# Forming the cross-attention factor G in three runs of 1536 columns for two batches, in place of four runs

## The chip, the cores and the metric

One core of one Trainium2 chip. The metric is the time of one execution on the device, in microseconds; lower is better. Spans in profiles are some 1.8 us shorter than these times.

## The reference, cut to what matters

```python
B, H, S, Ns, D = 8, 8, 512, 32, 64          # x [B,H,S,D], state [B,H,Ns,D]
a     = softmax(x @ state.T / sqrt(D))       # over the 32 states
xread = a @ state                            # 512 rows a batch
a2    = softmax(state @ x.T / sqrt(D))       # over the 512 tokens
sread = a2 @ x                               # 32 rows a batch
y = concat(xread, sread) as [B*(S+Ns), H*D]  # 4352 x 512
out = max(y @ w1, y @ w2, y @ w3) @ w_out    # 512 -> 768 -> 512
```

The kernel never forms xread. It forms G = state x (w1, w2, w3) of a batch, 2304 columns wide, and multiplies the softmax weights with it.

## The kernel before: what the change and the argument touch

Per batch b there are six "maxouts" (`x_maxout(b, m)`, 128 of the 768 columns of the maximum in the reference, 6 matmuls of 512 columns each), four "output pieces" of the batch ahead (`ffn_out(b-1, j)`, the product with w_out, 6 matmuls each), scores and softmax of batch b+1, `sread(b+1)`, and G, whose matmuls use the array as 8 tiles of 64 rows by 32 columns. A group of G is 8 such matmuls of up to 512 columns; a run is a stretch of groups with no other matmuls between. VectorE takes its instructions in the order of the program (in the prediction's lines softmax's reduction, at 79.20, stands between the maxima of two maxouts). The matmuls write to PSUM, from which the other engines copy. The kernel's PSUM tiles share buffers by tag: "two" has 2 buffers of 128x1024, "pw" has 4 of 128x512. A new tile waits until the last reader of the older tile in its buffer has ended.

```python
def g_front(b):                      # 1280 columns, beside sread
    flush_copies()
    g_piece(b, 0, 512, act)          # tag "two", copied out by ScalarE
    g_piece(b, 512, 1024, act, True) # True: ScalarE copies it one maxout later
    g_piece(b, 1024, 1280, dve)      # two tiles of tag "pw", copied by VectorE

def g_back(b):                       # 1024 columns, by itself
    flush_copies()
    g_piece(b, 1280, 1792, act)
    g_piece(b, 1792, 2304, act, True)

def maxout(b, m, n, lhs, rhs, nk):   # three tiles of "pw", released by these readers:
    ...
    nc.scalar.copy(out=t0[:, 0:n], in_=pw[0][:, 0:n])
    if copies_due:
        copies_due.pop(0)()
    nc.vector.tensor_max(t1[:, 0:n], t0[:, 0:n], pw[1][:, 0:n])
    nc.vector.tensor_max(ht[b][:, m, :], t1[:, 0:n], pw[2][:, 0:n])

for b in range(2, B):                # maxout m, then slots[m] in order
    n = b + 1
    slots = [[] for _ in range(NM)]
    if n < B:
        slots[0].append(lambda: scores(n, 0, 2))
        slots[1].append(lambda: softmax(n, 0, 2, (nc.gpsimd.tensor_mul, J)))
        slots[1].append(lambda: x_pad(n))            # GpSimd, for sread
        slots[2].append(lambda: a_transpose_dma(n))
        ...                                          # (cut)
    slots[1].append(lambda: g_back(b))
    if n < B:
        slots[4].append(lambda: sread(n))
        slots[4].append(lambda: g_front(n))
    for j, m in enumerate((1, 2, 4, 5)):             # output pieces: last in 1, 2; first in 4, 5
        slots[m].insert(0 if m > 2 else len(slots[m]), lambda j=j: ffn_out(b - 1, j))
    for m in range(NM):
        x_maxout(b, m)
        for f in slots[m]:
            f()
```

Maxouts 0 and 1 read the columns 0 to 768 of G, maxouts 2 and 3 those from 768 to 1536, maxouts 4 and 5 the rest.

The softmax here doesn't subtract the row's maximum and nothing guards it: scores larger than these inputs give would overflow.

## Time and profile before

| | before |
|---|---|
| time, median of 3 runs | 154.67 us |
| steady batch, start to start of maxout 0 | 15.21 us |
| runs of G for batches 2 to 7 | 12, of which 6 by themselves |
| copies of G in these batches | ScalarE 24 of 128x1024, VectorE 12 of 128x256 |

The prediction below shows the lines. PE is TensorE, PEld its weight loads, DVE VectorE, ACT ScalarE, POOL GpSimd. In the lists in order of time a line has the start in us, the length, the engine, the line of the kernel, what is written and read, and how many instructions are merged; a bracket at the end is the idle time of that engine just before, and what ended it. For TensorE only starts are to be compared, as the ends overlap the next instructions.

### The profile page before, as it was taken

How to read it: one execution, taken by the hardware profiler on the slowest of the kernel's cores; microseconds unless marked ns; L12 is line 12 of the kernel's file. 1: busy time of each engine (PE TensorE's matmuls, PEld its weight loads, DVE VectorE, ACT ScalarE, POOL GpSimd, SP SyncE). 2: the span in 40 equal slices, each digit the busy share in tenths (PEclk: the TensorE clock that was granted, in tenths of full speed). 3: DMA queues.
4: the chain of work that ended last, by engine and by line, in shares of the span. 5: the costliest groups of instructions: out<-in, count | busy, mean ns of one | idle time of the engine just before them, and what ended most of it. 6: DMA issues, size and time to landing. Idle time of an engine off the chain costs nothing.

```text
span 153.1 us, 3479 instructions
## 1 busy us (share of the span) xinstructions
PE 145.3 (95%) x1370; PEld 71.3 (47%) x1386; DVE 97.9 (64%) x177; ACT 93.9 (61%) x145; POOL 66.5 (43%) x80
## 2 busy tenths in 40 slices
PE   6988999999999999999999999999999999999990
PEld 2536543554453445344534453445344555665450
DVE  3477868768827685768576767776767684565110
ACT  3656878686948656865686568656865646333340
POOL 8977899754421782078308310821082100101050
PEclk9999999999999999999999999999999999999999
DMA  5999999999929999999496963061206120210374
GB/s 109 214 171 203 194 167 110 206 234 186 260 45 219 157 129 253 194 127 199 170 179 81 193 162 137 9 202 43 104 17 194 52 97 0 94 45 0 141 248 163
DMA packets 37376, 21.85 MB, mean 143 GB/s; under 512 B 22512, under 2 KB 35056, under 8 KB 37360
## 3 DMA queue, kind: packets, MB, share of 16 engines
q0 software_dynamic: 17184, 14.94, 52.4%
q1 hardware_dynamic: 19888, 6.43, 23.0%
q10 hardware_dynamic: 288, 0.26, 0.6%
q8 instruction: 11, 0.18, 0.5%
q14 instruction: 5, 0.04, 0.1%
HBM read 15.20 MB, written 8.91 MB: 158 GB/s over the span
## 4 chain that ended last, share of the span: by engine, by line
PE 84%; DMA 5%; POOL 4%; ACT 2%; issue 2%; DVE 0%; POOLq 0%
PE pw L373 44%; PE po L411 28%; DMA w<-in_moe_w_dram 5%; PE pg L301 4%; POOL w L109 2%; PE ps L200 2%; PE psr L267 2%; PE pg L327 2%; POOL x L80 2%; ACT G L333 1%; PE ph L403 1%; ACT t L377 1%; DVE t L380 0%; PE pat L231 0%; PE pxt L178 0%
## 5 line engine op out<-in xcount | busy, mean ns | idle before, releaser
L373 PE MATMUL pw<-aT,G 128*128 128x512 bf16 x288 | 69.0, 379 | 0.2 <-ACT G L333 0.2
L380 DVE TENSOR_TENSOR t<-t,pw 128x512 bf16<-128x512 bf16 (+1 forms) x54 | 35.1, 650 | 29.7 <-ACT t L377 29.6
L411 PE MATMUL po<-wout,ht 128*128 128x512 bf16 x183 | 46.6, 379 | 1.0 <-DVE t L380 0.2
L373 PEld LDWEIGHTS <-G 128*128 128x128 bf16 x288 | 26.8, 98 | 32.1 <-issue 2.7
L381 DVE TENSOR_TENSOR ht<-t,pw 128x512 bf16<-128x512 bf16 (+1 forms) x54 | 35.5, 658 | 5.6
L414 ACT COPY osb<-po 128x512 f32<-128x512 f32 x33 | 19.4, 586 | 29.6 <-PE po L411 29.6
L377 ACT CAST t<-pw 128x512 bf16<-128x512 f32 (+1 forms) x54 | 30.5, 565 | 10.4 <-PE pw L373 9.7
L411 PEld LDWEIGHTS <-ht 128*128 128x128 bf16 x198 | 18.8, 98 | 23.9 <-issue 2.8
L425 POOL DMA_DIRECT2D out_dram<-osb x14 | 7.9, 566 | 46.5 <-ACT osb L414 32.1
L220 POOL TENSOR_TENSOR a<-e,rden 128x1024 bf16<-128x1024 bf16 (+2 forms) x10 | 15.3, 1531 | 26.0 <-DVE rden L215 15.9
L308 ACT CAST G<-pg 128x1024 bf16<-128x1024 f32 x24 | 24.5, 1021 | 2.3 <-PE pg L301 1.5
L246 POOL COPY xp<-x 128x2048 bf16<-128x2048 bf16 x6 | 11.3, 1881 | 0.0
L213 DVE TENSOR_REDUCE den<-e 128x32 f32<-128x1024 bf16 (+1 forms) x10 | 9.9, 995 | 0.8 <-ACT e L205 0.8
L333 ACT CAST G<-pg 128x768 bf16<-128x768 f32 x11 | 8.7, 808 | 2.0 <-PE pg L327 2.0
L109 POOL DMA_DIRECT2D w<-in_moe_w_dram x12 | 9.2, 783 | 1.0 <-DVE rden L215 1.0
L373 PE MATMUL pw<-ats,w 128*128 128x256 bf16 x72 | 8.8, 273 | 0.0
L205 ACT ACTIVATE e<-ps 128x1024 bf16<-128x1024 f32 x6 | 6.2, 1029 | 3.7 <-PE ps L200 3.7
L127 PE MATMUL idle<-zero 128*128 128x512 bf16 x19 | 6.9, 512 | 1.2 <-DVE zero L85 1.2
L373 PEld LDWEIGHTS <-w 128*128 128x128 bf16 x72 | 7.0, 98 | 2.1
L301 PE MATMUL pg<-w,bd 64*32 64x512 bf16 x192 | 7.5, 381 | 0.0
L153 POOL COPY bd<-stT 64x512 bf16<-64x512 bf16 x6 | 6.5, 1082 | 0.9 <-DMA stT<-st 0.7
L200 PEld LDWEIGHTS <-xT 128*128 128x128 bf16 x128 | 5.0, 98 | 2.2 <-ACT xT L182 0.3
(61 smaller groups left out, 86.1 us busy)
## 6 DMA issues: line engine op xcount, KB each, us to landing
out_dram<-osb POOLq DMA_DIRECT2D x14, 512.0 KB, 3.2
x<-in_x_dram POOLq DMA_DIRECT2D x6, 512.0 KB, 9.2
w<-in_moe_w_dram POOLq DMA_DIRECT2D x6, 256.0 KB, 6.5
x<-in_x_dram POOLq DMA_DIRECT2D x3, 256.0 KB, 6.8
w<-in_moe_w_dram POOLq DMA_DIRECT2D x6, 128.0 KB, 7.0
wout<-in_moe_w_out_dram POOLq DMA_DIRECT2D x1, 768.0 KB, 11.1
x0f<-in_x_dram SPq DMA_DIRECT2D x1, 512.0 KB
out_dram<-osb SPq DMA_DIRECT2D x1, 512.0 KB, 2.7
```

Source lines behind the costliest of these rows:

```text
L109: nc.gpsimd.dma_start(out=w_slices(w_sb, c)[:, :, i, :], in_=w[:, :, m0 * 128:m1 * 128])
L220: mul(out=a[b][:, r, g0:g1].rearrange("p j g s n -> p j (g s) n"), in0=e[b][:, r, g0:g1].rearrange("p j g s n -> p j (g s) n"), in1=rden[: ...
L246: nc.gpsimd.tensor_copy(out=x_pads[b % 2][:, 2:2 + 2 * H * PW].rearrange("p (k c) -> p k c", c=PW)[:, :, 0:2 * D], in_=x_sb[b][:, 0:XW].re ...
L301: nc.tensor.matmul(ps[g][32 * s:32 * s + 32], bd(b, 2 * s + g)[64 * g:64 * g + 64, g, :], w_sb[64 * g:64 * g + 64, s, c0:c1], start=True, ...
L308: copy(out=G[b][:, :, c0:c1], in_=p[:, :, 0:n])
L333: copy(out=m_cols(G[b], m), in_=pv)
L373: nc.tensor.matmul(p[:, 0:n], lhs(i, k), rhs(k), start=(k == 0), stop=(k == nk - 1))
L377: nc.scalar.copy(out=t0[:, 0:n], in_=pw[0][:, 0:n])
L380: nc.vector.tensor_max(t1[:, 0:n], t0[:, 0:n], pw[1][:, 0:n])
L381: nc.vector.tensor_max(ht[b][:, m, :], t1[:, 0:n], pw[2][:, 0:n])
L411: nc.tensor.matmul(p, ht[b][:, m, j * 128:(j + 1) * 128], wout_sb[:, m, :], start=(m == 0), stop=(m == NM - 1))
L414: act(out=o[:, j, :], in_=p)
```

## The change

The intent: each change of TensorE between full-array matmuls and tiles of 64 by 32 costs time, so form G in runs as long as these buffers allow, 1536 columns, and need nine runs for six batches in place of twelve. The core of the diff (the body of the matmul loop, unchanged in substance, is cut):

```diff
+    def g_run(now, later, *split):
+        flush_copies()
+        for b, c0, c1 in (now, later):        # two tiles of tag "two", ScalarE copies
+            ...                               # (cut) `later` one maxout later
+        ps = [pp.tile([128, 512], F32, tag="pw", bufs=4, name=f"pgs{g}") for g in range(2)]
+        ...                                   # (cut) matmuls into ps
+        for g in range(2):
+            for b, c0, c1, r in placed:
+                dve(out=G[b][:, g, c0:c1], in_=ps[g][:, r])
+
+    def g_first(b):
+        g_run((b, 0, 512), (b, 512, 1024), (b, 1024, 1536))
+    def g_middle(b):
+        g_run((b, 1536, 2048), (b + 1, 0, 512), (b, 2048, 2304), (b + 1, 512, 768))
+    def g_last(b):
+        g_run((b, 1280, 1792), (b, 1792, 2304), (b, 768, 1280))
-    def g_front(b): ...
-    def g_back(b): ...
@@ before the loop
     x_pad(2)
+    x_pad(3)
@@
-    g_front(2)
+    g_first(2)
@@ in the loop
-            slots[1].append(lambda: x_pad(n))
+            if n + 1 < B:
+                slots[1].append(lambda: x_pad(n + 1))
@@
-        slots[1].append(lambda: g_back(b))
-        if n < B:
-            slots[4].append(lambda: sread(n))
-            slots[4].append(lambda: g_front(n))
+        if b % 2 == 0:
+            slots[2].append(lambda: sread(n))
+            slots[2].append(lambda: g_middle(b))
+        else:
+            slots[1].append(lambda: g_last(b))
+            if n < B:
+                slots[4].append(lambda: sread(n))
+                slots[4].append(lambda: g_first(n))
```

So even batches have sread and the middle run behind maxout 2, odd batches the last run behind maxout 1 and softmax, and sread with the first run of the next batch in slot 4.

More of the change, by code (lines that the diff above doesn't have):

```diff
@@ L287, in flush_copies, with g_matmuls @@
             copies_due.pop(0)()
-    def g_piece(b, c0, c1, copy, wait=False):
+    def g_matmuls(b, c0, c1, out):
         if c0 == 0:
             new(G, b, [128, 2, NM * 384], "G", bufs=3)
-        n = c1 - c0
-        if n > 256:
-            p = pp.tile([128, 2, 512], F32, tag="two", name="pg")
-            ps = [p[:, g, 0:n] for g in range(2)]
-        else:
-            ps = [pp.tile([128, n], F32, tag="pw", bufs=4, name=f"pgs{g}") for g in range(2)]
         for s in range(HS):
@@ L301, in g_piece, with place @@
                 nc.tensor.matmul(
-                    ps[g][32 * s:32 * s + 32],
+                    out(g)[32 * s:32 * s + 32],
                     bd(b, 2 * s + g)[64 * g:64 * g + 64, g, :], w_sb[64 * g:64 * g + 64, s, c0:c1],
                     start=True, stop=True, tile_position=(64 * g, 32 * s))
-        def place():
-            if n > 256:
-                copy(out=G[b][:, :, c0:c1], in_=p[:, :, 0:n])
-            else:
-                for g in range(2):
-                    copy(out=G[b][:, g, c0:c1], in_=ps[g])
-        if wait:
-            copies_due.append(place)
-        else:
-            place()
+    def g_run(now, later, *split):
+        flush_copies()
+        for b, c0, c1 in (now, later):
+            p = pp.tile([128, 2, 512], F32, tag="two", name="pg")
+            g_matmuls(b, c0, c1, lambda g: p[:, g])
+            def place(b=b, c0=c0, c1=c1, p=p):
+                act(out=G[b][:, :, c0:c1], in_=p)
+            if (b, c0, c1) == later:
+                copies_due.append(place)
+            else:
+                place()
+        ps = [pp.tile([128, 512], F32, tag="pw", bufs=4, name=f"pgs{g}") for g in range(2)]
+        at, placed = 0, []
+        for b, c0, c1 in split:
+            r = slice(at, at + c1 - c0)
+            at += c1 - c0
+            g_matmuls(b, c0, c1, lambda g: ps[g][:, r])
+            placed.append((b, c0, c1, r))
+        for g in range(2):
[7 more added lines that the diff above has]
+        g_run((b, 1280, 1792), (b, 1792, 2304), (b, 768, 1280))
     def g_cols(b, ms, copies=(act, act), defer=(False, False)):
@@ L338, in g_cols @@
                 place()
-    def g_front(b):
-        flush_copies()
-        g_piece(b, 0, 512, act)
-        g_piece(b, 512, 1024, act, True)
-        g_piece(b, 1024, 1280, dve)
-    def g_back(b):
-        flush_copies()
-        g_piece(b, 1280, 1792, act)
-        g_piece(b, 1792, 2304, act, True)
     def g_cols_fast(b, m):
```

## The prediction

> **What bounds the kernel now.** I read the page's busy times and its chain first, then TensorE in order of time over three steady batches, then VectorE in the same stretch, then the groups by shape. The page:
>
> ```profile
> PE 145.3 (95%) x1370; PEld 71.3 (47%) x1386; DVE 97.9 (64%) x177; ACT 93.9 (61%) x145; POOL 66.5 (43%) x80
> PE 84%; DMA 5%; POOL 4%; ACT 2%; issue 2%; DVE 0%; POOLq 0%
> ```
>
> TensorE is the bound: 95% busy, and 84% of the chain that ended last. VectorE and ScalarE have a third of the time free on average. TensorE in order of time, one batch b (start, length, then the instructions; starts are what counts, since matmuls overlap their tails):
>
> ```profile
> 74.25 1.46 PE L373 MATMUL pw<-aT,G 128*128 128x512 bf16 x6
> 75.55 0.63 PE L200 MATMUL ps<-bd,xT 128*128 128x64 bf16 x16
> 76.02 1.46 PE L373 MATMUL pw<-aT,G 128*128 128x512 bf16 x6
> 77.40 0.62 PE L301 MATMUL pg<-w,bd 64*32 64x512 bf16 x16
> 77.96 1.47 PE L411 MATMUL po<-wout,ht 128*128 128x512 bf16 x5
> 79.27 1.46 PE L373 MATMUL pw<-aT,G 128*128 128x512 bf16 x6
> ...
> 85.83 0.43 PE L267 MATMUL psr<-xp,e 128*32 128x65 bf16 x32
> 86.20 0.62 PE L301 MATMUL pg<-w,bd 64*32 64x512 bf16 x16
> 86.64 0.29 PE L301 MATMUL pgs<-w,bd 64*32 64x256 bf16 x8
> 86.86 1.47 PE L373 MATMUL pw<-aT,G 128*128 128x512 bf16 x6
> 89.46 1.46 PE L373 MATMUL pw<-aT,G 128*128 128x512 bf16 x6
> ```
>
> No line of this stretch carries an idle time, and the batch lasts 89.46 - 74.25 = 15.21 us. The six matmuls of a maxout or of an output piece take 1.29 us start to start, 0.216 each. The run of G at 77.40 is the back one: the maxout before it would have ended at 76.02 + 1.29 = 77.31, and the next output piece starts at 77.96. So 0.65 us for two groups of 512 columns, which stream in 0.43: **0.22 us is the price of one run's change into tiles of 64 by 32 and back.** Now VectorE over the same batch, maxouts 1 and 2 (L380 and L381 are the two maxima of a maxout, L213 and L215 are softmax of the next batch):
>
> ```profile
> 77.81 0.69 DVE L380 TENSOR_TENSOR t<-t,pw 128x512 bf16<-128x512 bf16 x1 [0.77 <-ACT t L377]
> 78.60 0.69 DVE L381 TENSOR_TENSOR ht<-t,pw 128x512 bf16<-128x512 bf16 x1
> 79.20 1.21 DVE L213 TENSOR_REDUCE den<-e 128x32 f32<-128x1024 bf16 x1
> 80.52 0.35 DVE L215 RECIPROCAL rden<-den 128x32 f32<-128x32 f32 x1
> 80.79 0.63 DVE L380 TENSOR_TENSOR t<-t,pw 128x512 bf16<-128x512 bf16 x1
> 81.52 0.69 DVE L381 TENSOR_TENSOR ht<-t,pw 128x512 bf16<-128x512 bf16 x1
> ```
>
> Here VectorE has no slack at all from 77.81 to 82.21; the instructions stand in the order of the program. That local crowd, not the 64%, decides this case. Last, what the copies of G cost, by shape:
>
> ```profile
> L308 ACT CAST G<-pg 128x1024 bf16<-128x1024 f32 x24 | 24.5, 1021 | 2.3 <-PE pg L301 1.5
> L311 DVE CAST G<-pgs 128x256 bf16<-128x256 f32 x12 | 4.5, 420 | 0.0
> L363 DVE CAST G<-pgf 128x384 bf16<-128x384 f32 x1 | 0.6, 558 | 0.2 <-PE pgf L358 0.2
> ```
>
> **What the Trainium skill says.** (1) "TensorEngine Tiling (Array Packing)", Tiling Modes, Key Properties: changing the tiling mode drains TensorE. The trace agrees: the 0.22 us above. (2) The same page, Performance Considerations, PSUM Bottleneck: tiling speeds up TensorE but not the emptying of PSUM. The trace agrees: a run of two groups streams in 0.43 us, while ScalarE takes 1.02 us to empty one group, 1024 elements a partition. (3) "TensorE: Matmul & The Clock Gate", Part 1, Architectural detail: ScalarE and VectorE are strict first-in first-out. The trace agrees: softmax's L213 runs between the maxima of maxouts 1 and 2, where the program puts it. (4) The same page, Part 1, HAM oscillation: gaps of TensorE over some 3.4 us lower its clock. The longest gap that I expect is about 2 us, so I expect the granted clock to stay; nothing in this trace tests it.
>
> **The change, part by part.**
>
> *Fewer runs (the gain).* Batches 2 to 7 have 12 runs now, 6 of them beside sread. After it there are 9: three times first, middle, last, and sread stands beside first and middle. Columns, matmuls and the six sreads stay. Three runs that stood alone go: 3 x 0.22 = 0.66 us off TensorE, all on the path.
>
> *Copies.* ScalarE loses 24 - 18 = 6 copies of 1.02 us. It is not on the path, so worth nothing. VectorE copies 128x256 twice a batch now; after, the first and last runs give it two copies of 128x512 each, the middle runs four of 128x256. A copy of 512 is an estimate from the two rows above: 420 ns at 256 and 558 at 384 make 696 at 512. The sum is small for VectorE (12 x 0.70 + 12 x 0.42 = 13.4 us against 4.5, some 70% of the span), but where do they stand?
>
> *The last run (odd b, after maxout 1).* Its VectorE part is columns 768 to 1280, which hold two thirds of the weights of maxout 2, and that maxout comes one output piece later. Before, those columns were formed in the front run, half a batch earlier. In slot 1 the copies are put after softmax, so VectorE reaches them where it reached L380 of maxout 2: 80.79. They end at 81.49 and, starting 0.61 later as independent instructions of 0.69 do in this trace, at 82.10. TensorE leaves the run at 77.96 + 0.22 = 78.18 (one more group) and would start maxout 2 at 79.47. The second matmul of maxout 2 needs the second copy (the half g = 1), then its weight load of 0.10: 82.24, so maxout 2 is as if started at 82.02. **Stall 2.55 us.** (The output piece between waits too, for the third buffer of tag pw, freed by the maximum that ends at 78.50; this lies inside the same 2.55.) It happens for b = 3 and 5. For b = 7 there is no softmax: VectorE is free at 126.1, the copies end at 127.4, maxout 2 is due at 127.3. About nothing.
>
> *The middle run (even b, after maxout 2).* Without a run in slot 1 TensorE comes 0.65 us sooner to maxout 2 (78.62 to 79.91), but VectorE doesn't, as softmax holds it. Then sread, the two pgs tiles and the next output piece want four buffers of tag pw, and there are four: the one of the output piece before and the three of maxout 2. Whatever order they are dealt in, the third waits for L380 of maxout 2 (ends 81.42) and the fourth for L381 (ends 82.21). Before, only the fourth tile after maxout 2 came near such a buffer, over 1.29 us later. TensorE reaches pgs at 79.91 + 0.09 + 0.36 + 0.44 = 80.80 and waits until 81.46: 0.66. It would be through at 81.68 and the output piece waits until 82.25: 0.57. **Stall 1.23 us**, for b = 2, 4 and 6. After it sread's small VectorE work and four copies of 256 end near 84.2, just before maxout 3 needs their buffers.
>
> *The first run.* It stands as the front one does. Its copies end near 88.31 instead of 87.76; the output piece after maxout 5 wants the buffer at 88.26. Stall 0.09 us, three times.
>
> *Padded copies.* Six as before, each one batch sooner. At the start the second of them may hold GpSimd up some 0.6 us before softmax of batch 2, whose product is needed a microsecond later than it is ready. Worth nothing.
>
> Sum: 2 x 2.55 + 3 x 1.23 + 3 x 0.09 - 0.66 = 5.10 + 3.69 + 0.27 - 0.66 = 8.4 us. 154.67 + 8.4 = 163.1; I say **163.0 us**.
>
> **The rivals.**
>
> *Only TensorE's work counts:* 154.0 us. For it: TensorE is the bound, VectorE is 64% busy, ScalarE gets lighter. Against it: the copies fall into the one stretch in which VectorE has no gap.
>
> *Only one of the two waits comes true.* If the last run's copies got ahead of softmax on VectorE (79.2 instead of 80.8), its stall would be 1.0 and the time 160; if the middle run's buffers came free sooner, 159.4. Against it: the order on VectorE in this trace is the program's, and four tiles in four buffers leave no choice.
>
> *Worse than the sum:* the stalls lower the granted clock, or push the output pieces and the next batch's transposed weights: 166 or more. For it: nothing in the trace but that the tail of a batch has less room. Against it: after each stall TensorE is late and the others have time to come back.
>
> **Range and chances.** The waits are worked out from starts that recur within 0.02 us in every batch, so the uncertainty is whether each exists, less its size. Losing half of the last run's stalls gives 160; a third more gives 165.5. Range 159.5 to 165.5. Slower by over 2% (above 157.8) needs some 3.8 of the 9.1 us of stalls: 0.92. Within 2%: 0.06. Faster by over 2% would need 3 us, five times what the runs can give: 0.02.
>
> **What would show each step.** Nine runs of G, three standing alone, and a run's change still 0.22: the gain. The line of TensorE's maxout 2 in odd batches with an idle time near 2 us whose releaser is the VectorE copy of G: the last run's stall. Pgs with an idle time near 0.6 released by L380, and the output piece after it near 0.5 released by L381: the middle's. The same start to start times of the groups elsewhere and PEclk at full: no other loss. ScalarE's copies of G at 18 and VectorE's busy share near 66% (its busy time up, over a longer span). I am wrong if odd batches start maxout 2 without a wait, or if a batch still takes near 15.1 us.

## The result, and the profile after

The time went from 154.65 us (median of 6 runs, 154.29 to 154.86) to 162.14 us (6 runs, 161.51 to 162.41). The ratio is 1.0481, 95% interval 1.0458 to 1.0504. A ratio here is the mean time of one kernel's fast runs over that of the other's of the same rounds, so not quite the ratio of the medians. The prediction was 163.0, range 159.5 to 165.5.

The page of the kernel after: busy times, the chain that ended last by engine, and two groups of copies of G (count, then busy us and mean ns of one).

```profile
PE 147.0 (92%) x1373; PEld 72.3 (45%) x1386; DVE 103.8 (65%) x189; ACT 88.0 (55%) x139; POOL 66.4 (42%) x80
PE 66%; DVE 14%; issue 5%; POOL 5%; DMA 4%; ACT 3%; DVEq 0%; ACTq 0%; POOLq 0%
L309 ACT CAST G<-pg 128x1024 bf16<-128x1024 f32 x18 | 18.3, 1018 | 4.4 <-PE pg L295 4.2
L324 DVE CAST G<-pgs 128x512 bf16<-128x512 f32 (+1 forms) x24 | 11.8, 543 | 0.3
```

Read the second line against its counterpart of before. VectorE had 0% of the chain and now has 14%, though its busy share is nearly the same. ScalarE lost its six copies. Nearly the whole loss is in two places. First the odd batches: TensorE of the kernel after in batch 5, from maxout 1 on (L379 a maxout, L295 G, L417 an output piece).

```profile
94.49 1.46 PE L379 MATMUL pw<-aT,G 128*128 128x512 bf16 x6
95.88 0.63 PE L295 MATMUL pg<-w,bd 64*32 64x512 bf16 x16
96.32 0.40 PE L295 MATMUL pgs<-w,bd 64*32 64x512 bf16 x8
97.02 1.46 PE L417 MATMUL po<-wout,ht 128*128 128x512 bf16 x5 [0.30 <-DVE t L386]
99.95 0.39 PE L379 MATMUL pw<-aT,G 128*128 128x512 bf16 x1 [1.47 <-DVE G L324]
100.54 1.25 PE L379 MATMUL pw<-aT,G 128*128 128x512 bf16 x5 [0.20 <-DVE G L324]
```

Maxout 2 (the last two lines) waits for VectorE's copy of G twice, once for each half. Without waits the output piece would start at 96.32 + 0.34 = 96.66 and maxout 2 at 97.95. Its second matmul comes at 100.54, so it is as if started at 100.33: a stall of 2.38 us. VectorE in the same stretch:

```profile
96.28 0.69 DVE L386 TENSOR_TENSOR t<-t,pw 128x512 bf16<-128x512 bf16 x1 [0.77 <-ACT t L383]
97.08 0.69 DVE L387 TENSOR_TENSOR ht<-t,pw 128x512 bf16<-128x512 bf16 x1
97.68 1.21 DVE L213 TENSOR_REDUCE den<-e 128x32 f32<-128x1024 bf16 x1
99.00 0.35 DVE L215 RECIPROCAL rden<-den 128x32 f32<-128x32 f32 x1
99.27 1.22 DVE L324 CAST G<-pgs 128x512 bf16<-128x512 f32 x2
```

The copies of G stand where the program puts them, behind softmax's reduction and reciprocal. G's matmuls were done near 97; its copies began at 99.27.

Second the even batches: TensorE of the kernel after in batch 4, from maxout 2 on (L267 is sread).

```profile
81.17 1.46 PE L379 MATMUL pw<-aT,G 128*128 128x512 bf16 x6
82.56 0.44 PE L267 MATMUL psr<-xp,e 128*32 128x65 bf16 x32
...
83.37 0.27 PE L295 MATMUL pgs<-w,bd 64*32 64x256 bf16 x1
84.03 0.41 PE L295 MATMUL pgs<-w,bd 64*32 64x256 bf16 x15 [0.40 <-DVE t L386]
84.83 1.45 PE L417 MATMUL po<-wout,ht 128*128 128x512 bf16 x5 [0.38 <-DVE ht L387]
86.12 2.75 PE L379 MATMUL pw<-aT,G 128*128 128x512 bf16 x12
88.85 1.46 PE L417 MATMUL po<-wout,ht 128*128 128x512 bf16 x6
```

The second tile of pgs waits for the first maximum of maxout 2, the output piece for the second maximum: both are the readers whose end frees a buffer of tag pw. The bracket counts only the time in which nothing ran. From starts, pgs at 83.37 with 16 matmuls would have let the output piece start at 83.70, and it started at 84.83: 1.13 us. The last line starts 2.73 us after the twelve matmuls before it, which take 2.59: another 0.14. The line names no releaser. ScalarE's copy in maxout 4 ends at 88.18 + 0.62 = 88.80, just before 88.85, so that copy's buffer is the likely one; no run tests it.

The bookkeeping closes. A pair of batches took 92.73 - 58.90 = 33.83 us against 2 x 15.21 = 30.42: 3.41 us more, and 2.38 + 1.13 + 0.14 less one run's 0.22 is 3.43. The time in the profiles before batch 2 differs too: its first maxout starts at 43.06 us here and at 43.83 before. TensorE of the kernel before waits 0.69 us for a load of x at 9.24; in this one execution it does not. That comes long before the first edited instruction, and sread(2) starts anywhere from 37.0 to 38.1 us in the traces of the thirteen kernels told here, so the change is hardly behind it.

### The profile page after: what moved, and what is told of

It reads as the page before. It is cut to its first block, busy times and chain, and to the rows that moved or that the text cites. A ratio compares the mean times of both kernels' runs of the same rounds, so it can differ in the third digit from the quotient of the medians.

```text
span 159.7 us, 3484 instructions
## 1 busy us (share of the span) xinstructions
PE 147.0 (92%) x1373; PEld 72.3 (45%) x1386; DVE 103.8 (65%) x189; ACT 88.0 (55%) x139; POOL 66.4 (42%) x80
## 4 chain that ended last, share of the span: by engine, by line
PE 66%; DVE 14%; issue 5%; POOL 5%; DMA 4%; ACT 3%; DVEq 0%; ACTq 0%; POOLq 0%
PE pw L379 35%; PE po L417 23%; DMA w<-in_moe_w_dram 4%; DVE den L213 4%; DVE ht L387 4%; DVE t L386 4%; POOL w L109 2%; ACT t L383 2%; DVE G L324 2%; PE ps L200 2%; PE pg L344 2%; POOL x L80 2%; PE pg L295 1%; PE psr L267 1%; PE ph L409 1%
## 5 line engine op out<-in xcount | busy, mean ns | idle before, releaser
L379 PE MATMUL pw<-aT,G 128*128 128x512 bf16 x288 | 69.3, 379 | 3.5 <-DVE G L324 3.3
L417 PE MATMUL po<-wout,ht 128*128 128x512 bf16 x186 | 46.6, 379 | 2.5 <-DVE ht L387 1.1
L379 PEld LDWEIGHTS <-G 128*128 128x128 bf16 x288 | 26.9, 98 | 36.3 <-DVE G L324 5.2
L417 PEld LDWEIGHTS <-ht 128*128 128x128 bf16 x198 | 19.1, 97 | 24.9 <-issue 4.2
L309 ACT CAST G<-pg 128x1024 bf16<-128x1024 f32 x18 | 18.3, 1018 | 4.4 <-PE pg L295 4.2
L324 DVE CAST G<-pgs 128x512 bf16<-128x512 f32 (+1 forms) x24 | 11.8, 543 | 0.3
L379 PE MATMUL pw<-ats,w 128*128 128x256 bf16 x72 | 8.8, 273 | 0.0
L379 PEld LDWEIGHTS <-w 128*128 128x128 bf16 x72 | 7.0, 98 | 2.1
```

The source lines that it names most:

```text
L309: act(out=G[b][:, :, c0:c1], in_=p)
L324: dve(out=G[b][:, g, c0:c1], in_=ps[g][:, r])
L379: nc.tensor.matmul(p[:, 0:n], lhs(i, k), rhs(k), start=(k == 0), stop=(k == nk - 1))
L417: nc.tensor.matmul(p, ht[b][:, m, j * 128:(j + 1) * 128], wout_sb[:, m, :], start=(m == 0), stop=(m == NM - 1))
```

## The experiments

Each experiment was timed in turns with the kernel before on the same chip; the first four shared a chip. Where an edit is to another experiment's kernel it says so.

### The last run ahead of softmax

```diff
-            slots[1].append(lambda: g_last(b))
+            slots[1].insert(0, lambda: g_last(b))
```

> The changed kernel with one edit: the last run of G (odd batches) stands ahead of softmax in slot 1, so its two VectorE copies are queued ahead of softmax's reduction and reciprocal. My theory (the copies wait behind softmax): in the changed kernel's trace they start at 99.27 and maxout 2 is as if started at 100.33 where 97.95 was possible, a stall of 2.38 us. Ahead of softmax they start near 97.68, when the second maximum of maxout 1 has gone through, and end near 98.95; maxout 2 is as if started at 98.8: stall near 0.9 in batches 3 and 5, 1.5 us less each, so 162.1 - 3.0 = 159.1 us. Rival (the copies are slow in themselves, or the wait is for ScalarE's copy or for buffers): no change, 162 us.

Measured: 159.39 us against 154.40 before, ratio 1.0306 (1.0261 to 1.0351). TensorE of this kernel in batch 5, the output piece and maxout 2:

```profile
95.60 1.45 PE L417 MATMUL po<-wout,ht 128*128 128x512 bf16 x6 [0.30 <-DVE t L386]
97.00 0.39 PE L379 MATMUL pw<-aT,G 128*128 128x512 bf16 x1
97.60 1.25 PE L379 MATMUL pw<-aT,G 128*128 128x512 bf16 x5 [0.21 <-DVE G L324]
```

The 1.47 us in front of the first matmul are gone. Maxout 1 starts at 93.07 here, so the second matmul of maxout 2 comes 4.53 us after it, against 100.54 - 94.49 = 6.05 in the changed kernel: 1.52 us less, as worked out. Place in VectorE's queue was two thirds of this stall. Of the 0.85 left, some 0.36 is the output piece's wait for the first maximum of maxout 1 (pgs starts at 94.90 in this trace, so that the output piece could start at 95.24), and the rest is the two copies themselves.

### The middle run behind the output piece

```diff
-            slots[2].append(lambda: sread(n))      # in the even branch
-            slots[2].append(lambda: g_middle(b))
+            pass
@@ after the loop that places ffn_out
+        if b % 2 == 0:
+            slots[2].append(lambda: sread(n))
+            slots[2].append(lambda: g_middle(b))
```

> The changed kernel with one edit: in even batches sread and the middle run stand behind the output piece of slot 2, not ahead of it. My theory (four tiles at once out of four buffers, two of which VectorE frees late): TensorE reaches pgs 1.29 us later, when the maxima of maxout 2 are nearly done; by the starts of the changed kernel's trace there remain about 0.15 us before pgs and 0.3 before the third tile of maxout 3 and the first of maxout 4, against 1.13 + 0.14 now. 0.8 us less in each of three batches: 162.1 - 2.4 = 159.7 us. Rival (the stall comes from the run itself, its four copies or the padded x, wherever it stands): no change, 162 us. Second rival (the wait only moves behind the run, as the copies then meet maxout 3): 161 to 162 us, with idle times on the first matmuls of maxouts 3 and 4.

Measured: 159.07 us against 154.40, ratio 1.0292 (1.0256 to 1.0328). TensorE of this kernel in batch 4, pgs, then maxouts 3 and 4, then the output piece:

```profile
84.06 0.57 PE L295 MATMUL pgs<-w,bd 64*32 64x256 bf16 x16
84.56 2.83 PE L379 MATMUL pw<-aT,G 128*128 128x512 bf16 x12
87.25 1.46 PE L417 MATMUL po<-wout,ht 128*128 128x512 bf16 x6
```

Of 1.27 us there remain 84.56 - 84.06 - 0.33 = 0.17 at pgs and 87.25 - 84.56 - 2.59 = 0.10 at maxouts 3 and 4. The run, its columns and its four copies are the same, so the run itself is not the cost. Four tiles asked of four buffers, just when VectorE is late, are.

### Both

The two edits together.

> Both edits: last run ahead of softmax, middle run behind the output piece. If the two stalls are separate, the gains add: 162.1 - 3.0 - 2.4 = 156.7 us, still slower than before by 2 us. If they share a cause further up (VectorE late as a whole), the sum is less than the parts: 158 us or more.

Measured: 156.30 us against 154.40, ratio 1.0106 (1.0072 to 1.0140). The gains of the single edits, 162.14 - 159.39 = 2.8 and 162.14 - 159.07 = 3.1, add to 5.9; together they gave 162.14 - 156.30 = 5.8. The two stalls are separate. By the starts, 2 x 0.85 + 3 x 0.27 - 0.66 = 1.85 us remain in this trace, and 156.30 - 154.40 = 1.90 were measured. (The 162.14 was measured at another time, so these sums hold to some tenths.)

### Other columns for VectorE in the last run

```diff
-            if (b, c0, c1) == later:
+            if (b, c0, c1) == later and c0 != 1280:      # copy both at once
@@
-        g_run((b, 1280, 1792), (b, 1792, 2304), (b, 768, 1280))
+        g_run((b, 768, 1280), (b, 1280, 1792), (b, 1792, 2304))
```

> The changed kernel with one edit in the last run: ScalarE takes the columns 768 to 1792 that maxouts 2 and 3 need, both copies at once, and VectorE the columns 1792 to 2304 that maxout 4 needs; VectorE's copies stay behind softmax. It takes the data wait away and leaves the buffers of tag pw held by pgs as long as now. If only the data wait counts, the stall falls from 2.38 to the 0.30 of the output piece: 162.1 - 4.2 = 157.9 us. If the buffers count too, as I think, the second tile of maxout 2 waits for the copy out of the output piece (0.5), the third for the first pgs (0.4) and the next output piece for the second (0.1): stall near 1.25, 162.1 - 2.2 = 159.9 us.

Measured: 159.15 us against 154.40, ratio 1.0307 (1.0262 to 1.0352); between the two numbers, nearer to the one that counts buffers. TensorE of this kernel in maxout 2 of batch 3:

```profile
65.07 0.59 PE L379 MATMUL pw<-aT,G 128*128 128x512 bf16 x2 [0.24 <-ACT osb L420]
65.87 0.59 PE L379 MATMUL pw<-aT,G 128*128 128x512 bf16 x2 [0.20 <-DVE G L324]
```

Maxout 2 no longer needs what VectorE copies, and yet its third tile waits for VectorE's copy: it needs that copy's buffer. (The edit also takes away the delay of ScalarE's second copy, so it is not a change of VectorE's columns alone.) A late copy out of PSUM is paid for as data or as a buffer.

### The padded copies alone

The kernel before with only the two `x_pad` edits of the diff.

> The kernel before with only the padded copies of x one batch sooner (GpSimd copies for batches 2 and 3 back to back, then each a batch ahead). My theory: nothing waits for them, same time as before within 0.3 us. Rival (GpSimd's copies a batch sooner disturb VectorE or softmax's product): over 1 us slower.

Measured: 154.26 us against 154.20, ratio 1.0014 (0.9986 to 1.0042). This part of the change costs nothing that shows.

### Six more runs

To measure the price of a run, the kernel before with its back run cut in two:

```diff
     def g_back(b):
         flush_copies()
         g_piece(b, 1280, 1792, act)
-        g_piece(b, 1792, 2304, act, True)
+    def g_rest(b):
+        flush_copies()
+        g_piece(b, 1792, 2304, act, True)
@@ after the loop that places ffn_out
+        slots[2].append(lambda: g_rest(b))
```

> The kernel before with the back run cut in two: the columns 1792 to 2304 are formed in a run of their own ahead of maxout 3, so 18 runs of G in place of 12, the same matmuls and the same copies. My theory (a run that stands alone costs 0.22 us of TensorE for the change of tiling): 6 x 0.22 = 1.3 us slower, ratio 1.0085. Rival (the change of tiling is hidden, the gap lies in something else): ratio 1.000. If waits for copies come on top, TensorE's lines show idle times and the ratio is above 1.010.

Measured: 158.44 us against 154.20, ratio 1.0263 (1.0238 to 1.0289), three times the expected loss. The trace has the reason: twice as much as the run costs is lost at maxout 4, whose matmuls wait for ScalarE's copy of just these columns (from starts, maxouts 3 and 4 take 86.44 - 83.37 = 3.07 us in place of 2.59: 0.48 a batch). I had given that copy too little time. So the run was moved to the end of the batch ahead (`slots[5].append(lambda: g_rest(n))`, and `g_rest(2)` ahead of the loop):

> The kernel before with the columns 1792 to 2304 formed in a run of their own at the end of the batch ahead: 18 runs in place of 12, as in six_more_runs, but the copy has three microseconds more before maxout 4 needs it. six_more_runs was 4.1 us slower; by its trace 0.24 us a batch is the run's change of tiling and 0.46 a wait of maxout 4 for that copy. Here the wait should go and 6 x 0.24 = 1.4 us stay: ratio 1.009, 1.008 to 1.012 with small waits. If the price of a run is less than 0.15 us, ratio under 1.006.

Measured: 155.95 us against 154.28, ratio 1.0125 (1.0095 to 1.0155). TensorE of this kernel around the added run (in its own line numbers L414 is the output piece, L301 G, L376 the maxout):

```profile
72.65 1.46 PE L414 MATMUL po<-wout,ht 128*128 128x512 bf16 x6
74.04 0.41 PE L301 MATMUL pg<-w,bd 64*32 64x512 bf16 x8
74.38 1.47 PE L376 MATMUL pw<-aT,G 128*128 128x512 bf16 x6
```

The output piece's six matmuls end at 72.65 + 1.29 = 73.94; G starts 0.10 later, and the maxout 0.34 later, of which 0.216 are the group's columns. In and out: 0.22 us. The batch takes 15.44 us here against 15.21. So the price of a run is 0.22 to 0.23, read twice. Six of them make 1.4 us, 0.9%; the measured 1.25% is somewhat more. The trace has no place for the rest: from sread(2) to the last product (`ph`) it has 148.49 - 37.35 = 111.14 us against 147.84 - 38.12 = 109.72, which is 1.42 more. But the execution that was profiled took 155.38 us, the fastest of the six, so the rest stays open.

### Nine runs where VectorE has room

```diff
-    x_pad(3)                                    # and padded copies as before the change
@@ before the loop, behind ffn_out(0, 3)
+    g_middle(2)
@@ in the loop
         if b % 2 == 0:
-            slots[2].append(lambda: sread(n))
-            slots[2].append(lambda: g_middle(b))
-        else:
-            slots[1].append(lambda: g_last(b))
-            if n < B:
-                slots[4].append(lambda: sread(n))
-                slots[4].append(lambda: g_first(n))
+            slots[4].append(lambda: sread(n))
+            slots[4].append(lambda: g_last(n))
+        elif n < B:
+            slots[4].append(lambda: sread(n))
+            slots[4].append(lambda: g_first(n))
@@ after the loop that places ffn_out
+        if b % 2 and n < B:
+            slots[5].append(lambda: g_middle(n))
```

> Nine runs as in the changed kernel, with the same columns in each, but where VectorE has room: the last run beside sread in slot 4 of even batches, the first beside sread in slot 4 of odd batches, the middle one by itself at the end of odd batches; padded copies as before the change. My theory: no stall over 0.1 us is left, so the 3 runs less show: 3 x 0.22 = 0.66 us faster than before, ratio 0.996, or 0.998 with small waits. Rival (nine runs of 1536 columns cost by themselves, by VectorE's larger share of the copies): slower than before by over 1%.

Measured: 155.09 us against 154.20, ratio 1.0059 (1.0041 to 1.0077). The expectation missed. (Its rival, a loss of over 1%, did not come either.) No large stall is left, but TensorE at maxouts 3 and 4 of batch 4 shows a small one:

```profile
82.08 2.99 PE L379 MATMUL pw<-aT,G 128*128 128x512 bf16 x12
84.91 1.46 PE L417 MATMUL po<-wout,ht 128*128 128x512 bf16 x6
```

The twelve matmuls take 84.91 - 82.08 = 2.83 us in place of 2.59. With no run of G in slot 1, TensorE reaches maxout 3 sooner by the 0.65 us of that run, but VectorE, with softmax in its queue, does not free maxout 2's buffers sooner. The lone run of the kernel before was in part a cover for softmax: taking it away there gives back some 0.2 us of what it costs, in most batches. By the starts, batches 2 to 6 lose 1.03 us between maxout 1 and the end of maxout 4, and maxout 0 behind the three middle runs 0.25 more. Less 0.66 that is 0.6 us, which is what this trace has (110.30 us from sread(2) to the last product against 109.72); 0.9 were measured.

### Softmax in two halves, or later

On that kernel, `softmax(n, 0, 1, ...)` in slot 1 and `softmax(n, 1, 2, ...)` in slot 2 ahead of the transpose of the weights:

> The kernel run_elsewhere with softmax's reduction and reciprocal in two halves, one behind maxout 1 and one behind maxout 2. The run before this was 0.6% slower than before where 0.4% faster was expected; its trace shows why: in batches without a run of G in slot 1, TensorE comes 0.65 us sooner to maxouts 2 and 3 while VectorE is held by softmax, and maxouts 3 and 4 take 2.79 to 2.83 us in place of 2.59. If that is the whole of it, halving softmax lets the maxima of maxout 2 through 0.65 us sooner, the 0.2 us a batch go, and the time comes 1.0 to 1.3 us down, to 153.9: ratio 0.996 to 0.999. If the nine runs cost for another reason, the ratio stays at 1.006.

Measured: 156.39 us against 154.41, ratio 1.0129 (1.0104 to 1.0154). Half of it came true: maxouts 3 and 4 of batch 4 took 84.45 - 81.86 = 2.59 us again. But the padded copy, in slot 1, now stood between softmax's two products on GpSimd. TensorE of this kernel at maxout 0 of batch 5:

```profile
91.72 1.47 PE L379 MATMUL pw<-aT,G 128*128 128x512 bf16 x6 [1.98 <-DMA aT<-a]
```

The transposed weights of the next batch came late. Moving all of softmax to slot 2 had the same fault and kept the small stall (the twelve matmuls took 2.81 us):

> The kernel run_elsewhere with the whole of softmax behind maxout 2 in place of maxout 1, ahead of the maxima of maxout 3. By the starts in run_elsewhere's trace the wait at maxout 3 goes, and the first maximum of maxout 3 comes about 0.5 us late, which the second tile after it may feel by 0.1 to 0.3 us. Ratio 0.998 to 1.006. Slower than run_elsewhere would say that the crowd on VectorE only moves.

Measured: 158.74 us against 154.41, ratio 1.0283 (1.0256 to 1.0309), a miss: I had looked at VectorE's room alone and not at how late the weights may be.

Last, the halves with the padded copies one batch sooner, behind the second half:

```diff
+    x_pad(3)                                    # ahead of the loop, behind x_pad(2)
-            slots[1].append(lambda: x_pad(n))
+            if n + 1 < B:
+                slots[2].append(lambda: x_pad(n + 1))
             slots[2].append(lambda: a_transpose_dma(n))
```

> softmax_halves with the padded copies one batch sooner and behind the second half's product on GpSimd. softmax_halves took the waits at maxouts 3 and 4 away (2.59 us again), but its padded copy stood between the two products on GpSimd, so the transposed weights came late and maxout 0 waited 2.1 us in batch 5, 0.3 in batch 3. With the copies out of the way nothing should wait: two batches took 32.43 us there with a wait of 2.15, so 30.28 against 30.42 before; three such pairs make 0.4 us: ratio 0.996 to 0.998, the first version faster than before. If the transposed weights are still late (SyncE's queue, not GpSimd): 1.005 or more, with idle times released by the transposing DMA.

Measured: 154.08 us against 154.28, ratio 0.9983 (0.9959 to 1.0006). The expected 0.996 to 0.998 is just missed. Nine runs without a large stall are as fast as the kernel before and perhaps a trace faster; the interval does not exclude no gain at all. Two batches take 90.64 - 60.27 = 30.37 us in its trace (scores to scores) against 30.42. One run less should make it 30.20. The other 0.17 us is two small waits: maxout 0 behind the middle run takes 75.89 - 74.50 = 1.39 us in place of 1.30, a weight load in it released by VectorE's copy of G, and the next batch's maxout 0 comes 89.34 - 87.96 = 1.38 after the output piece, its weight load released by the transposed weights. So the price of a run is gained here too, and most of it lost again.

## Why the prediction was right

Term by term, as the prediction has them.

- **The last run: 2 x 2.55, measured 2 x 2.38.** The wait, its place, its releaser and the batches (3 and 5, none in 7) were as predicted, and the experiment that moved the copies ahead of softmax took away the 1.5 us that their place in the queue should cost. Too large by 0.17: I added 0.10 for the weight load after the copy, but the trace has the weight load and the matmul both starting at 100.54, 0.05 after the copy ends. The Trainium skill has it so ("TensorE: Matmul & The Clock Gate", Part 1, Architectural detail: a matmul can begin before its weight load completes), and I had missed it. And the two copies took 1.22 us, not 1.31 (674 ns each on average, not 696).
- **The middle run: 3 x 1.23, measured 3 x (1.13 + 0.14).** Both waits and both releasers were as predicted. I took pgs as one group of 256 columns where it has two, so the unstalled start of the output piece was 0.11 us too early and the stall 0.1 too large. The 0.14 at the next output piece was not foreseen.
- **The first run: 3 x 0.09, measured nothing.** The output piece after maxout 5 starts 1.30 us after it (75.52 - 74.22), as before. VectorE's copies end at 74.35 + 1.29 = 75.64, so it did not wait for their buffer, as I had it.
- **Fewer runs: 3 x 0.22, confirmed** by 0.23 a run in the kernel with six more.
- **Padded copies: nothing, confirmed.**
- **Starts that recur within 0.02 us in every batch:** true of TensorE, not of VectorE. The first maximum of maxout 2 comes 6.54 us after its batch's start in batches 3, 4 and 6 of the kernel before, but 6.47 in batch 2 and 6.75 in batch 5. This did no harm here.

With the measured terms the sum is 4.76 + 3.81 - 0.66 = 7.9 us, against 7.5 between the medians; the prediction's was 8.4. The two traces have 7.74 between sread(2) and the last product (154.73 - 37.27 = 117.46 us against 109.72), so the sum is 0.2 too large there, some of it in batch 2, whose first wait is shorter (0.33 us idle at pgs in place of 0.40). The rest stays open: it lies in the start and the end, which vary from execution to execution (in these two they were 0.85 and 0.29 us shorter in the kernel after). In the middle run's term two misses nearly cancel, 0.1 too much and 0.14 not foreseen; that its size came out so near is luck.

Of the rivals, "only TensorE's work counts" is refuted: the idle lines of the two stretches name VectorE. "Only one of the two waits" is refuted by the two single edits, each of which took away its own. "Worse than the sum" did not come: the granted clock was 1.00 in the stretches of the traces that hold the gaps, 1.47 us here and 1.98 in the kernel with softmax in halves. No gap came near the 3.4 us of the prediction's point (4), so no run here tests that.

The prediction had one more thing right that I then forgot. It says that without a run in slot 1 TensorE comes 0.65 us sooner to maxout 2 and VectorE, held by softmax, does not, and it counts that for the middle run. My expectation for the well-placed nine runs did not, and so took the 0.66 us as clear gain. In the kernel before, VectorE used the time of the lone run to get through softmax.

## What to carry to other kernels

Ask of each job that you merge or move not only what it costs on the engine that bounds the kernel, but where its copies land in the queue of the engine that empties PSUM, and what stands ahead of them there: VectorE at 64% had no room at all for 4.4 us of the batch shown. When a tile comes out of PSUM late, someone waits for its data or for its buffer, so count the tiles that are asked for at once against the buffers and the time at which the oldest reader ends. And a stretch of work that looks like overhead may be covering another engine's; taking it away is then worth less than its length.

## What the Trainium skill lacked or had wrong

- "TensorEngine Tiling (Array Packing)", Tiling Modes, Key Properties, says that a change of the tiling mode drains TensorE but gives no price. Here one run in tiles of 64 by 32 between full matmuls cost 0.22 to 0.23 us, 0.10 going in and 0.12 coming out. The runs show the price, not the drain itself.
- The same page, Performance Considerations, PSUM Bottleneck, advises using ScalarE and VectorE both for emptying PSUM. It does not say that it counts what stands ahead in the engine's queue: on VectorE two copies of 0.67 us stood behind 1.6 us of softmax, and moving them ahead gave back 1.52 of a stall of 2.38 us.
